# Moving some inverse roots from GpSimd to ScalarE, reordering the first loads, the residual adds and the w_down loads in a linear-attention kernel

## The chip, the core and the metric

The kernel runs on one core of one Trainium2 chip. The metric is the device time of one execution in microseconds (us), the median of several executions. Lower is better. A profile of one execution shows what every engine did: TensorE (PE for its matmuls, PEld for its weight loads), VectorE (DVE), ScalarE (ACT), GpSimd (POOL), and SyncE (SP), which here only issues DMAs. Each engine works through its own instructions in order; semaphores tie them together.

## The reference

The input `x` has 2048 rows of 640 numbers, in bf16. The output is the sum of `x`, of a linear attention and of a small expert branch, both on the normalised rows:

```python
x = A_x
xn = _layernorm(x, axis=-1)            # (x - m) / sqrt(v + 1e-5)
return x + _A_ref(xn, A_wqkv, A_wo) + _B_ref(xn, B_w_r, B_w_gate, B_w_up, B_w_down)

# _A_ref: 32 heads of width 20; phi(t) = where(t > 0, t + 1, exp(t)) + 1e-6
q, k, v = split(x @ wqkv);  pq, pk = phi(q), phi(k)
kv = einsum("bhsd,bhse->bhde", pk, v);  z = einsum("bhsd->bhd", pk)
o = einsum("bhqd,bhde->bhqe", pq, kv) / (einsum("bhqd,bhd->bhq", pq, z) + 1e-6)
return o @ wo

# _B_ref: the 8 rows with the largest router score go through a gated expert
r = x @ w_r;  idx = argsort(-r)[:8];  x_sel = x[idx]
y = (silu(x_sel @ w_gate) * (x_sel @ w_up)) @ w_down * sigmoid(r[idx])
return x.at[idx].add(y)
```

## The kernel before

The 2048 rows are 16 tiles of 128 rows, numbered 0 to 15; a tile's rows lie on the 128 partitions. The program is written out in order (a manual schedule), so the order of the statements is each engine's order. All loads of the long middle part are issued by SP, in the order of the text.

**Start.** ScalarE issues the two pieces of the k weight (`wk`, L88) and the router vector (L89), and then loads its function table (L90). SP issues x tiles 0, 1 and 2 (L92). `load_rest` (L93 to L102) issues the other x tiles and the q weight; its first load waits for a small GpSimd memset.

**Normalisation of a tile.** `stat` (L178) gives mean and variance on VectorE. Then the inverse root of the variance is needed, and there are two helpers for it: `root_act` (L183) does it with two small ScalarE instructions, Ln and Exp, and `root_pool` (L188) with two small GpSimd instructions, an add (L190) and a power (L191). `norm_dve` (L199) or `norm_pool` (L205) writes the normalised tile `xn`. Tiles 0 to 4 are transposed by TensorE (`tr_pe`) and copied out of PSUM by ScalarE and VectorE (`tr_ev`, L234); tiles 5 to 15 by a DMA transpose that SP issues (`tr_dma`, L243). Before, tiles 0 and 1 take their root from ScalarE and tiles 2 to 15 from GpSimd. From tile 5 on, odd tiles are normalised by VectorE and even ones by GpSimd.

**The middle loop** (L481 to L513) has a step for each tile t from 5 to 15. In step t TensorE does the k product of tile t (`k_half` twice), in some steps a unit of the q product (`q_mm`), and the product of the normalised tile t-4 with its phi(k) (`g1`, L279). ScalarE takes exp and relu of k and q from PSUM (`k_act`, `q_act`), VectorE joins them (`k_phi`, L272, and `q_phi`, L302). The same step prepares tile n = t+4: statistics, root, normalisation, transpose. For odd n the normalisation stands at the head of the following step. Weight loads are issued between the steps (`w_jobs`), among them `w_gate`, `w_up`, `wv`, `wo` and four pieces of `w_down` (`load_wd`).

**The residual.** `adds` (L473) turns tiles of `x_sb` in place into x plus its normalised value, with one GpSimd instruction for each tile (`add_s`, L220) and one small one for each group (L474). They stand in steps 12 to 15 and behind the loop (L525). `load_s` (L107) then stores the sums in four pieces to a scratch area in HBM; the last two pieces of `w_down` are issued behind these stores (L528).

**Behind the loop** the router's 8 rows are found, mostly on VectorE, ending with the row numbers `idx_i` (L574). GpSimd gathers the 8 columns into `xsT` (L575 to L577), TensorE does the expert products (L714 with gate and up, L747 with `w_down`), and an indirect DMA adds the result to the scratch area (L763), which is read back into `x_sb` (L768). The last part multiplies each tile by the folded output matrix (`o_mm`, L795) and adds `x_sb`.

Of the kernel before, what the change touches and what calls it, by code (L numbers as in the profile page):

```python
# [37 lines left out]
def kernel(  # L38
# [45 lines left out]

    SP = nc.sync
    wr5 = sb("wr5", [KC, P])
    for lo, hi in ((0, 3), (3, 5)):
        A.dma_start(wk[:, lo:hi, 0:D], wqkv_v[:, lo:hi, D : 2 * D])  # L88
    A.dma_start(wr5[:], B_w_r.rearrange("(kc p) -> kc p", p=P))  # L89
    A.preload_act_table_set("natural_log_exp_and_others")  # L90
    for t in range(3):
        SP.dma_start(x_sb[:, t, :], x_v[:, t, :])  # L92
    def load_rest():  # L93

        G.memset(x_sb[0:1, 3, 0:1], 0.0)
        SP.dma_start(x_sb[:, 3, :], x_v[:, 3, :])
        for a in (4, 6):
            SP.dma_start(x_sb[:, a : a + 2, :], x_v[:, a : a + 2, :])
        SP.dma_start(x_sb[:, 8:12, :], x_v[:, 8:12, :])
        for lo, hi in ((0, 3), (3, 5)):  # L100
            SP.dma_start(wq[:, lo:hi, :], wqkv_v[:, lo:hi, 0:D])
        SP.dma_start(x_sb[:, 12:16, :], x_v[:, 12:16, :])  # L102
# [52 lines left out]
    def router_col():  # L155
        PE.transpose(psb[:, 6, 512 : 512 + KC], wr5[:], ident[0:KC, 0:KC])
        A.copy(wk[:, :, D], psb[:, 6, 512 : 512 + KC])
# [30 lines left out]
    def root_pool(t, n=1):  # L188
        sl = slice(t, t + n)
        G.tensor_scalar_add(t2[:, sl], mv[:, sl, 1], EPS_BF16)  # L190
        G.tensor_tensor(out=rs[:, sl], in0=t2[:, sl], in1=mhalf[:, 0:n], op=ALU.pow)  # L191
# [7 lines left out]
    def norm_dve(t):  # L199
        V.tensor_scalar(  # L200
            out=xn[:, t, :], in0=x_sb[:, t, :], scalar1=mv[:, t, 0:1], scalar2=rs[:, t : t + 1],
            op0=ALU.subtract, op1=ALU.mult,
        )
# [30 lines left out]
    def tr_ev(t, other=A):  # L234
        dst = xnT[:, :, t * P : (t + 1) * P]
        A.copy(dst[:, 0:3, :], psb[:, 7, 0 : 3 * P].rearrange("p (k f) -> p k f", k=3))
        src = psb[:, 6, 0 : 2 * P].rearrange("p (k f) -> p k f", k=2)
        if other is A:
            A.copy(dst[:, 3:, :], src)
        else:  # L240
            V.tensor_copy(dst[:, 3:, :], src)
# [6 lines left out]
    def k_half(t, b):  # L248
        b0 = K_BANK.get(t, 0)
        n = HW + (b if t else 0)  # L250
        for kc in range(KC):
            PE.matmul(  # L252
                ps[:, b0 + b, 0:n],
                lhsT=xnT[:, kc, t * P : (t + 1) * P],
                rhs=wk[:, kc, b * HW : b * HW + n],
                start=(kc == 0), stop=(kc == KC - 1),
            )
# [3 lines left out]
    def k_act(t):  # L261
        b0 = K_BANK.get(t, 0)
        e = evk.tile([P, 2, HW], BF16, tag="ek", name=f"ek{t}")
        r = evk.tile([P, 2, HW], BF16, tag="rk", name=f"rk{t}")
        for b in range(2):
            A.activation(e[:, b, :], ps[:, b0 + b, 0:HW], AF.Exp)  # L266
            A.activation(r[:, b, :], ps[:, b0 + b, 0:HW], AF.Relu)  # L267
        if t:
            A.copy(r_all[:, t : t + 1], ps[:, b0 + 1, HW : HW + 1])
        kev[t] = e, r  # L270
# [39 lines left out]
    def q_ev(u, bank=7):  # L310
        q_act(u, bank)
        q_phi(u)
# [91 lines left out]
    stat(2, 0)  # L404
    norm_dve(1)
    stat(2, 1)
    root_pool(2)
    const_iota()
    k_half(0, 0)
    tr_pe(1)  # L410
    k_half(0, 1)
    tr_ev(1, V)
    router_col()
    k_act(0)
    stat(3, 0)
# [40 lines left out]
    k_half(4, 0)  # L456
    q_act(0)
    k_half(4, 1)
    norm_dve(7)
    tr_dma(7)  # L460
    k_act(4)
    k_phi(3)
    stats2(8)
    root_pool(8)
    norm_pool(8)
# [7 lines left out]
    def adds(t, n):  # L473
        G.tensor_scalar_add(rs1[:, t : t + n], rs[:, t : t + n], 1.0)  # L474
        for i in range(t, t + n):
            add_s(i)

    q_at = {5: (2, 3), 6: (4,), 8: (5,), 10: (6,), 12: (7,)}
    later = {12: [const_grep], 13: [copy_grep]}
    add_at = {12: (0, 2), 13: (2, 2), 14: (4, 3), 15: (7, 3)}  # L480
    for t in range(5, T):  # L481
        qs = q_at.get(t, ())
        n = t + 4
        if 9 < n <= T and n % 2 == 0:
            norm_dve(n - 1)
            tr_dma(n - 1)
            shift(n - 1, 1)
        if qs:
            q_mm(qs[0])
        k_half(t, 0)  # L490
        k_half(t, 1)
        if n < T:
            stats2(n)
            root_pool(n)
            if n % 2 == 0:
                norm_pool(n)
                tr_dma(n)
        if qs:
            q_ev(qs[0])
        k_act(t)  # L500
        if len(qs) > 1:
            q_mm(qs[1])
        g1(t - 4)
        k_phi(t)
        if len(qs) > 1:
            q_ev(qs[1])
        for job in w_jobs.pop(t - 4, []) + later.pop(t, []):
            job()
        if t == 5:
            shift(0, 6)  # L510
            shift(7, 1)
        if t in add_at:
            adds(*add_at[t])  # L513
# [8 lines left out]
                    start=(t == 0 and c in (0, 4)), stop=(t == T - 1), skip_group_check=True,  # L522
                )

    adds(10, 6)  # L525
    for a in range(0, T, 4):
        load_s(a)
    for i in sorted(w_jobs):  # L528
        for job in w_jobs[i]:
            job()  # L530
    PE.transpose(psb[0:T, 1, 0:P], r_all[:], ident[:])
    g1(T - 4)
    r_row = sb("r_row", [T, P], F32)
# [343 lines left out]
```

## Time and profile before

| quantity | value |
|---|---|
| median of 3 runs | 120.12 us (119.82 to 121.27) |
| the profiled execution's own time | 120.3 us |
| its span on the core | 118.6 us |
| granted TensorE clock over the span | 0.999 |
| busy: PE, DVE, ACT, POOL | 108.1, 83.6, 63.6, 51.7 us |
| moved by DMA | 21.77 MB |

The span runs from the first to the last instruction on the core; the 1.7 us between it and the run's own time lie around it. Busy time is an average over stages that have different limits, so the waits are read stage by stage. A row of the timeline gives the start, the duration, the engine, the line, the operation with output and input, the count of merged instructions, and in brackets the idle time before it with what ended it.

### The profile page before, as it was taken

The page shows a single profiled execution, that of the slowest core. Times are in us where ns is not written, and L with a number is a line of the kernel's source. Part 1 is how long each engine was busy: PE and PEld are TensorE (multiplying, and loading weights), DVE is VectorE, ACT ScalarE, POOL GpSimd, SP SyncE. Part 2 cuts the span into 40 slices and gives each one's busy share as a digit, 9 for nine tenths or more (in the row PEclk, how much of TensorE's full clock was granted, in tenths as well). Part 3 has the DMA queues.
Part 4 walks back from the last instruction along what each step waited for, and adds up shares of the span by engine and source line. Part 5 has one row for each costly group of instructions (what it writes and reads, how often), then busy time and mean ns, then how long its engine had stood idle before and what let it go on. Part 6 is the DMA issues. An engine that isn't in the chain of part 4 may idle for free.

```text
span 118.6 us, 2512 instructions
## 1 busy us (share of the span) xinstructions
PE 108.1 (91%) x902; PEld 63.4 (53%) x912; DVE 83.6 (71%) x176; ACT 63.6 (54%) x156; POOL 51.7 (44%) x99
## 2 busy tenths in 40 slices
PE   5778899999999859799999998999999999999980
PEld 2145464546565435365445956665445566677760
DVE  3498797999949495822609959987776568875570
ACT  1438899658585825566219465575977466300000
POOL 7207668283857669899999922000500000000000
PEclk9999999999999999999999999999999999999999
DMA  3999805505827999999999999700059932243333
GB/s 57 377 346 365 283 15 57 112 6 87 288 55 214 276 159 343 249 255 253 182 192 215 378 380 269 128 0 6 3 153 378 358 111 89 94 154 113 114 116 108
DMA packets 22240, 21.77 MB, mean 184 GB/s; under 512 B 8555, under 2 KB 20947, under 8 KB 22227
## 3 DMA queue, kind: packets, MB, share of 16 engines
q1 hardware_dynamic: 20361, 19.58, 61.6%
q10 hardware_dynamic: 1834, 2.01, 4.9%
q8 instruction: 7, 0.11, 0.4%
q14 instruction: 6, 0.05, 0.1%
q0 software_dynamic: 32, 0.01, 0.1%
HBM read 14.42 MB, written 5.25 MB: 166 GB/s over the span
## 4 chain that ended last, share of the span: by engine, by line
PE 29%; DVE 19%; DMA 19%; POOL 17%; issue 7%; ACT 3%; POOLq 2%; SPq 1%
PE ps L795 18%; DMA s_dram<-x_sb 10%; POOL rs L191 7%; DVE stats L179 5%; DMA wv<-in_A_wqkv_dram 5%; PE ps L289 5%; POOL xn L211 4%; POOL t L190 4%; DVE xn L200 4%; DVE pqT L305 4%; DMA x_sb<-in_A_x_dram 4%; DVE pk L274 2%; POOLq L576 2%; DVE mv L181 2%; PE ps L653 2%
## 5 line engine op out<-in xcount | busy, mean ns | idle before, releaser
L252 PE MATMUL ps<-wk,xnT 128*128 128x320 bf16 (+1 forms) x160 | 25.0, 300 | 2.5 <-DMA xnT<-xn 2.4
L289 PE MATMUL ps<-xnT,wq 128*128 128x512 bf16 x93 | 24.0, 379 | 0.7 <-issue 0.2
L795 PE MATMUL ps<-late,pqT 128*128 128x320 bf16 x150 | 21.3, 299 | 0.0
L252 PEld LDWEIGHTS <-xnT 128*128 128x128 bf16 x160 | 15.0, 97 | 11.1 <-DMA xnT<-xn 3.4
L298 ACT ACTIVATE eq<-ps 128x512 bf16<-128x512 f32 x20 | 12.0, 598 | 15.2 <-PE ps L289 15.1
L281 PE MATMUL ps<-pk,xn 128*128 128x512 bf16 x77 | 19.4, 379 | 0.2
L266 ACT ACTIVATE ek<-ps 128x320 bf16<-128x320 f32 x32 | 14.4, 449 | 7.3 <-PE ps L252 7.3
L795 PEld LDWEIGHTS <-pqT 128*128 128x128 bf16 x150 | 14.3, 98 | 6.2 <-issue 0.4
L274 DVE SCALAR_TENSOR_TENSOR pk<-ek,rk 128x640 bf16<-128x640 bf16 x16 | 13.4, 846 | 5.8 <-ACT rk L267 5.7
L804 DVE TENSOR_TENSOR o<-ps,x_sb 128x640 bf16<-128x640 f32 x15 | 12.3, 823 | 6.5 <-PE ps L795 5.6
L305 DVE SCALAR_TENSOR_TENSOR pqT<-eq,rq 128x512 bf16<-128x512 bf16 x20 | 14.1, 706 | 3.9 <-ACT rq L299 3.9
L222 POOL TENSOR_SCALAR x_sb<-x_sb,rs,nm 128x640 bf16<-128x640 bf16 x16 | 15.9, 1008 | 0.5
L179 DVE BATCH_NORM_STATS2 stats<-x_sb 128x6 f32<-128x320 bf16 x32 | 14.4, 481 | 2.3 <-DMA x_sb<-in_A_x_dram 2.3
L289 PEld LDWEIGHTS <-wq 128*128 128x128 bf16 x100 | 9.3, 97 | 10.6 <-issue 1.0
L267 ACT ACTIVATE rk<-ps 128x320 bf16<-128x320 f32 x32 | 14.5, 454 | 0.0
L190 POOL TENSOR_SCALAR t<-mv 128x1 bf16<-128x1 f32 x14 | 5.7, 410 | 15.0 <-DVE mv L181 14.6
L299 ACT ACTIVATE rq<-ps 128x512 bf16<-128x512 f32 x20 | 11.9, 593 | 0.0
L281 PEld LDWEIGHTS <-xn 128*128 128x128 bf16 x80 | 7.6, 97 | 7.6
L191 POOL TENSOR_TENSOR rs<-t,mhalf 128x1 f32<-128x1 bf16 x14 | 10.5, 753 | 1.2
L200 DVE TENSOR_SCALAR xn<-x_sb,mv,rs 128x640 bf16<-128x640 bf16 x11 | 5.3, 479 | 5.8 <-POOL rs L191 5.7
L611 ACT CAST spare<-ps 128x1024 bf16<-128x1024 f32 (+1 forms) x7 | 6.0, 896 | 3.2 <-PE ps L600 3.2
L831 ACT CAST o<-ps 128x160 bf16<-128x160 f32 x1 | 0.3, 292 | 12.7 <-PE ps L821 12.7
(125 smaller groups left out, 114.4 us busy)
## 6 DMA issues: line engine op xcount, KB each, us to landing
s_dram<-x_sb SPq DMA_DIRECT2D x4, 640.0 KB, 9.1
x_sb<-s_dram SPq DMA_DIRECT2D x4, 640.0 KB, 6.8
wd<-in_B_w_down_dram SPq DMA_DIRECT2D x4, 480.0 KB, 9.0
wg<-in_B_w_gate_dram SPq DMA_DIRECT2D x2, 768.0 KB, 4.9
wu<-in_B_w_up_dram SPq DMA_DIRECT2D x2, 768.0 KB, 5.1
x_sb<-in_A_x_dram SPq DMA_DIRECT2D x2, 640.0 KB, 8.4
out_dram<-o SPq DMA_DIRECT2D x8, 160.0 KB, 1.8
out_dram<-o ACTq DMA_DIRECT2D x7, 160.0 KB, 1.8
```

What stands on the lines that cost most here:

```text
L179: V.bn_stats(out=stats[:, t, b, :], in_=x_sb[:, t, b * HW : (b + 1) * HW])
L191: G.tensor_tensor(out=rs[:, sl], in0=t2[:, sl], in1=mhalf[:, 0:n], op=ALU.pow)
L222: G.tensor_scalar(out=x_sb[:, t, :], in0=x_sb[:, t, :], scalar1=rs1[:, sl], scalar2=nm[:, sl], op0=ALU.mult, op1=ALU.add,)
L252: PE.matmul(ps[:, b0 + b, 0:n], lhsT=xnT[:, kc, t * P : (t + 1) * P], rhs=wk[:, kc, b * HW : b * HW + n], start=(kc == 0), stop=(kc == KC ...
L266: A.activation(e[:, b, :], ps[:, b0 + b, 0:HW], AF.Exp)
L267: A.activation(r[:, b, :], ps[:, b0 + b, 0:HW], AF.Relu)
L274: V.scalar_tensor_tensor(out=pk[:, t, :].rearrange("p (b f) -> p b f", b=2), in0=e[:], scalar=1.0, in1=r[:], op0=ALU.min, op1=ALU.add,)
L281: PE.matmul(ps[:, 2 + c, :], lhsT=xn[:, t, c * P : (c + 1) * P], rhs=pk[:, t, 0:512], start=(t == 0), stop=(t == T - 1),)
L289: PE.matmul(ps[:, bank, :], lhsT=wq[:, kc, m * P : (m + 1) * P], rhs=xnT[:, kc, tb * 512 : (tb + 1) * 512], start=(kc == 0), stop=(kc == K ...
L305: V.scalar_tensor_tensor(out=pqT[:, m, tb * 512 : (tb + 1) * 512], in0=e[:], scalar=1.0, in1=r[:], op0=ALU.min, op1=ALU.add,)
L795: PE.matmul(ps[:, b0 + b, 0:HW], lhsT=pqT[:, kc, t * P : (t + 1) * P], rhs=Ms[:, kc, b * HW : (b + 1) * HW], start=(kc == 0), stop=(kc == ...
L804: V.tensor_tensor(out=o_t[:], in0=ps[:, b0 : b0 + 2, 0:HW], in1=x_sb[:, t, :].rearrange("p (b f) -> p b f", b=2), op=ALU.add,)
```

## The change

- The first x tiles: ScalarE issues x tile 1 and then the first piece of `wk`; SP issues x tiles 0 and 2, then the second piece of `wk`, then the router vector.
- Roots: tile 2 takes its root from ScalarE, behind `tr_ev(1)`. In the loop, odd tiles (9, 11, 13, 15) take it from ScalarE at the end of the step, even ones from GpSimd as before. Tiles 3 to 8 stay on GpSimd.
- In front of the loop, `k_act(4)` and `k_phi(3)` stand ahead of `norm_dve(7)` and its transpose.
- The residual adds: one tile each in steps 7, 9 and 11, two in steps 12 and 13, three in 14 and 15, and three behind the loop in place of six.
- The last two pieces of `w_down` are issued ahead of the four stores.

```diff
-    for lo, hi in ((0, 3), (3, 5)):
-        A.dma_start(wk[:, lo:hi, 0:D], wqkv_v[:, lo:hi, D : 2 * D])
-    A.dma_start(wr5[:], B_w_r.rearrange("(kc p) -> kc p", p=P))
+    A.dma_start(x_sb[:, 1, :], x_v[:, 1, :])
+    A.dma_start(wk[:, 0:3, 0:D], wqkv_v[:, 0:3, D : 2 * D])
     A.preload_act_table_set("natural_log_exp_and_others")
-    for t in range(3):
+    for t in (0, 2):
         SP.dma_start(x_sb[:, t, :], x_v[:, t, :])
+    SP.dma_start(wk[:, 3:5, 0:D], wqkv_v[:, 3:5, D : 2 * D])
+    SP.dma_start(wr5[:], B_w_r.rearrange("(kc p) -> kc p", p=P))
...
     stat(2, 1)
-    root_pool(2)
     const_iota()
...
     tr_ev(1, V)
+    root_act(2)
     router_col()
...
     k_half(4, 1)
+    k_act(4)
+    k_phi(3)
     norm_dve(7)
     tr_dma(7)
-    k_act(4)
-    k_phi(3)
...
-    add_at = {12: (0, 2), 13: (2, 2), 14: (4, 3), 15: (7, 3)}
+    add_at = {7: (0, 1), 9: (1, 1), 11: (2, 1), 12: (3, 2), 13: (5, 2), 14: (7, 3), 15: (10, 3)}
...
             stats2(n)
-            root_pool(n)
             if n % 2 == 0:
+                root_pool(n)
                 norm_pool(n)
                 tr_dma(n)
...
         if len(qs) > 1:
             q_ev(qs[1])
+        if n < T and n % 2:
+            root_act(n)
...
-    adds(10, 6)
-    for a in range(0, T, 4):
-        load_s(a)
+    adds(13, 3)
     for i in sorted(w_jobs):
         for job in w_jobs[i]:
             job()
+    for a in range(0, T, 4):
+        load_s(a)
```

## The prediction

> **What bounds the kernel now.** I read the busy times first, then the waits of TensorE, and then a table of stretches, because a wait only counts where TensorE stands still for it.
>
> ```profile
> span 118.6 us, 2512 instructions
> PE 108.1 (91%) x902; PEld 63.4 (53%) x912; DVE 83.6 (71%) x176; ACT 63.6 (54%) x156; POOL 51.7 (44%) x99
> ```
>
> ```profile
> PE ps L252 <- DMA xnT<-xn: 2.4, 2, 1.6
> PE ps L230 <- DVE xn L200: 1.8, 3, 1.2
> PE ps L714 <- POOL xsT L577: 0.4, 1, 0.4
> ...
> DVE xn L200 <- POOL rs L191: 5.7, 6, 1.7
> ```
>
> ```profile
> 0.00:6.46 6.46, 4.02 (x10) 1.19 (x10) 3.11 (x9) 1.78 (x3) 2.96 (x20) 1.00 0.72 229
> 6.46:15.60 9.14, 8.34 (x72) 5.09 (x73) 7.62 (x24) 6.98 (x22) 4.38 (x15) 1.00 0.88 304
> 15.60:41.00 25.40, 25.05 (x140) 13.63 (x140) 20.87 (x49) 18.74 (x56) 16.94 (x26) 1.00 0.51 125
> 41.00:50.00 9.00, 6.50 (x38) 3.56 (x39) 7.62 (x15) 4.12 (x14) 6.86 (x10) 1.00 1.07 247
> 50.00:75.00 25.00, 24.33 (x299) 14.80 (x299) 15.11 (x37) 13.34 (x31) 18.96 (x29) 1.00 1.10 263
> 75.00:115.30 40.30, 39.89 (x354) 25.10 (x353) 29.24 (x47) 18.36 (x33) 1.61 (x1) 1.00 0.39 129
> ```
>
> The columns of the waits are the total, the number and the longest; those of the stretches are from:to, length, busy time of PE, PEld, DVE, ACT and POOL, granted clock, DMA share and GB/s. TensorE is busy 25.05 of 25.40 us, 24.33 of 25.00 and 39.89 of 40.30, so three stretches can hardly be shortened by this change, which leaves its work as it is. It stands still in three places: at the start until 6.46 and a little up to 15.60 (9.14 less 8.34 is 0.80 us), from 41 to 50 (2.5 us, for two DMA transposes), and 0.4 us for the gather at L714. Whatever the change is worth must come out there.
>
> **The change part by part.**
>
> *The first tiles.*
>
> ```profile
> 3.62 0.89 DVE L179 BATCH_NORM_STATS2 stats<-x_sb 128x6 f32<-128x320 bf16 x2 [1.47 <-DMA x_sb<-in_A_x_dram]
> ...
> 4.85 0.29 ACT L185 ACTIVATE lg<-mv,eps 128x1 f32<-128x1 f32 x1 [1.11 <-DVE mv L181]
> 5.18 0.20 ACT L186 ACTIVATE rs<-lg 128x1 f32<-128x1 f32 x1
> ...
> 5.56 0.49 DVE L179 BATCH_NORM_STATS2 stats<-x_sb 128x6 f32<-128x320 bf16 x1 [0.81 <-DMA x_sb<-in_A_x_dram]
> 5.97 0.43 DVE L200 TENSOR_SCALAR xn<-x_sb,mv,rs 128x640 bf16<-128x640 bf16 x1
> ```
>
> Tile 0's root is ready at 5.18 + 0.20 = 5.38, but its normalisation starts at 5.97, because VectorE does tile 1's statistics first and waited 0.81 us for tile 1 until 5.56. Issued first on the other queue, tile 1 no longer stands behind tile 0 and a k weight piece. The statistics then fit right behind tile 0's, which end near 4.8 (3.62 + 0.89 and a sum of 0.21), in the time of the root, and the normalisation starts at about 5.45: 0.52 us sooner. If both tiles now share the engines evenly, tile 0 lands later, at worst at the mean of the two old times, (3.62 + 5.56) / 2 = 4.59, which is 0.97 later and makes this term -0.45. At best tile 0 lands sooner too; the gain has the end 1.47, the whole idle time of the first row. I take 0.52, the row it is nearest to, since tile 0 is still the first of SP's queue. The k weight's second piece now stands behind two x tiles on SP: before, the first k product waited for ScalarE's copy and not for a weight:
>
> ```profile
> 7.37 0.52 PEld L252 LDWEIGHTS <-xnT 128*128 128x128 bf16 x5 [0.52 <-ACT xnT L236]
> ```
>
> The bytes ahead of it on both queues together stay the same, so I cost it at nothing; if that cover is gone, TensorE waits here for the weight. The router vector goes behind it and is needed by one transpose after that product. SP's next load, tile 3, waits for a GpSimd memset as before.
>
> *The root of tile 2.*
>
> ```profile
> 8.66 0.48 ACT L236 COPY xnT<-ps 128x384 bf16<-128x384 bf16 x1 [0.92 <-PE ps L230]
> 9.30 0.58 POOL L191 TENSOR_TENSOR rs<-t,mhalf 128x1 f32<-128x1 bf16 x1
> 9.91 0.67 DVE L200 TENSOR_SCALAR xn<-x_sb,mv,rs 128x640 bf16<-128x640 bf16 x1 [0.45 <-POOL rs L191]
> ```
>
> On the old clock, ScalarE ends its copy at 8.66 + 0.48 = 9.14; Ln and Exp by the rows above take 0.29 + 0.20, with three hand-overs of 0.04 (5.14 to 5.18) it is 9.75, against 9.91: 0.16 sooner. The normalisation took 0.67, against 0.43 for tile 0's, while GpSimd built its index constants beside it; those constants now run sooner, as GpSimd has no root of tile 2 to wait for. That gives up to 0.24 more, together 0.4. Behind the two instructions on ScalarE stand the router's copy and tile 0's exp and relu, which TensorE needs only at tile 3. I take 0.4 of the 0.80 us in which TensorE still waits in this stretch; the ends are 0 and 0.8.
>
> The Trainium skill, "SBUF — State Buffer", section "Summary: rules for kernel authors", has it that a VectorE instruction in a two-port mode and a GpSimd instruction block each other for the whole instruction. The pair 0.67 and 0.43 agrees, and by that rule the residual adds in steps 7, 9 and 11 would lie in front of VectorE in return.
>
> *Tile 7 and phi(k) of tile 3.*
>
> ```profile
> 20.34 0.57 POOL L191 TENSOR_TENSOR rs<-t,mhalf 128x1 f32<-128x1 bf16 x1
> 20.95 0.45 DVE L200 TENSOR_SCALAR xn<-x_sb,mv,rs 128x640 bf16<-128x640 bf16 x1 [0.77 <-POOL rs L191]
> 21.31 0.82 DVE L274 SCALAR_TENSOR_TENSOR pk<-ek,rk 128x640 bf16<-128x640 bf16 x1
> ```
>
> VectorE waited 0.77 us for GpSimd's root, and phi(k) came after. Now phi(k), which needs nothing new, fills that wait; the root is ready at 20.91 as before, so what follows comes 0.7 us sooner. VectorE's waits in this stretch are mostly those for GpSimd's roots (5.7 us in six), and the next of them comes after tile 10's statistics, so these start 0.52 + 0.4 + 0.7 = 1.6 us sooner. The ends for this step are 0 and 0.77.
>
> *The transposes.*
>
> ```profile
> 28.61 0.87 DVE L179 BATCH_NORM_STATS2 stats<-x_sb 128x6 f32<-128x320 bf16 x2
> 31.93 1.56 POOL L211 TENSOR_SCALAR xn<-x_sb,rs,nm 128x640 bf16<-128x640 bf16 x1
> 33.52 1.20 SPq L244 DMA_TRANSPOSE xnT<-xn  x1
> 34.48 0.45 DVE L200 TENSOR_SCALAR xn<-x_sb,mv,rs 128x640 bf16<-128x640 bf16 x1 [1.74 <-POOL rs L191]
> 34.77 1.08 SPq L105 DMA_DIRECT2D wg<-in_B_w_gate_dram  x2
> 35.95 5.08 SPq L244 DMA_TRANSPOSE xnT<-xn  x2
> 42.73 1.21 PEld L252 LDWEIGHTS <-xnT 128*128 128x128 bf16 x10 [2.12 <-DMA xnT<-xn]
> ...
> 49.69 0.39 PEld L252 LDWEIGHTS <-xnT 128*128 128x128 bf16 x4 [1.31 <-DMA xnT<-xn]
> ```
>
> This is the chain to see. Tile 11's root is what VectorE waits 1.74 us for, and that wait goes; but tile 11 is normalised at 34.93 and its transpose is issued at 35.95, because SP first issues tile 10's transpose (33.52, at the end of 31.93 + 1.56 = 33.49) and two weight pieces. Tile 10 has an even number: its root stays on GpSimd. So the removed wait is not what frees TensorE at 42.73. What moves that transpose is tile 10's statistics at 28.61, 1.6 us sooner by the sum above. The transpose of tile 11 then lands at about 42.73 - 1.6 = 41.1. TensorE would be there at 42.73 - 1.6 (its longest wait) - 0.9 (the first two terms) = 40.2, still waits 0.9, and goes on 1.6 us sooner than before. The other wait, 2.4 - 1.6 = 0.8 us at 49.69, is for tile 13, behind two pieces of `w_up`. Here the earlier root helps, since tile 12's statistics follow tile 11's normalisation; but the transfers ahead keep their length. Its ends are 0 and 0.8; I take 0.2, nearer to the transfers.
>
> *What ScalarE takes on.* Five roots at 0.49 are 2.5 us. ScalarE is busy 18.74 of 25.40, so they find room; behind each stand the next exp and relu, for which TensorE waits last. GpSimd loses five roots and gets three more small sums.
>
> *The adds and the gather.*
>
> ```profile
> 61.78 5.61 POOL L222 TENSOR_SCALAR x_sb<-x_sb,rs,nm 128x640 bf16<-128x640 bf16 x6
> 65.40 0.15 DVE L574 CAST idx_i<-cols 128x1 int32<-128x1 f32 x1
> 67.34 1.27 POOL L577 COPY xsT<-xnT 128x5 bf16 x3
> 73.34 1.42 PEld L714 LDWEIGHTS <-xsT 128*32 128x32 bf16 x40 [0.69 <-POOL xsT L577]
> ```
>
> The gather starts at 67.34, behind the sixth add, though the row numbers are there at 65.55. Three adds at 5.61 / 6 = 0.93 are gone from here, 2.8 us, so the gather starts 67.34 - 65.55 = 1.8 us sooner against its neighbours. TensorE's wait for it is only 0.4, so 0.4 is the gain; then TensorE's own work is next. The expert's last product waits for nothing but its weight loads and the chain before it:
>
> ```profile
> 79.30 0.81 PEld L747 LDWEIGHTS <-late 128*32 128x32 bf16 x48
> ```
>
> No wait for `w_down` is shown, so its earlier issue gains nothing. The stores go behind it; their user, the indirect add, comes after L747, 12 us after the last add at 67.39, which covers them.
>
> *Sum.* 0.52 + 0.4 + 0.7 + 0.2 + 0.4 = 2.2 us off the profiled run's 120.3 gives 118.1. That run stands 0.2 above the median of 120.12, from which the same sum gives 117.9. I predict **118.0 us**. From no change this kernel's measurement can tell about 2%, here 117.7 and 122.5.
>
> **The rivals.**
>
> *All the waits go.* If the DMA queue has a gap that the earlier issue closes, tile 13's transpose keeps up: 2.2 + 0.6 = 2.8, and if tile 11's remaining 0.9 goes too, 3.7: 116.5 to 117.4, say 117.0. For it speaks the DMA share of 0.51 before 41; against it 1.07 after.
>
> *The late statistics stay where they are.* If VectorE gives back the 0.7 at tile 7, for the three adds put beside it (3 x 0.93 = 2.8 us of GpSimd) or for GpSimd's slow pieces, the transposes come only 0.9 sooner: 0.9 + 0.4 = 1.3, 118.9. For it speaks the 1.56 us normalisation, against 0.93 for an add of the same size; against it VectorE's 1.74 us of idle time in the later steps.
>
> *The change does not do what it says at the start.* Tile 0 shares the sixteen DMA engines with tile 1 and lands later; between the ends 0.52 and -0.45 that is a term near 0, and 118.5. The Trainium skill, "DMA: Bandwidth & Descriptors", section "Issuing engines are not separate DMA queues", says that transfers issued by several engines run on the same DMA engines and interleave, so that only issue time is saved. By that rule this case would be the likelier one for tile 0; the trace of before has no two x tiles in flight on two queues and does not decide it.
>
> *Slower than before: ScalarE is held up by its new waits.*
>
> ```profile
> 30.90 0.43 ACT L267 ACTIVATE rk<-ps 128x320 bf16<-128x320 f32 x1
> 31.84 0.21 DVE L181 BATCH_NORM_AGGREGATE mv<-stats 128x2 f32<-128x12 f32 x1
> 32.73 0.60 ACT L298 ACTIVATE eq<-ps 128x512 bf16<-128x512 f32 x1 [1.34 <-PE ps L289]
> ```
>
> At the end of step 7 ScalarE is done at 31.33, tile 11's variance is there at 32.05, and ScalarE's next work at 32.73. Ln and Exp fit in by 0.2 us. If the variance comes later, Ln stops everything behind it: the q and k pieces in PSUM stay, and TensorE cannot refill the banks. Some 0.5 us more pass before that hurts. Four tiles with a variance 1.25 us later would cost 4 x (1.25 - 0.7) = 2.2 and eat the gain; with 1.5 us it is 3.2, and the run takes 121.1. VectorE's place in the order ahead of phi(k) of the step speaks against it.
>
> **How the numbers follow.** The forecast has 0.45 (117.5 to 118.6), all waits gone 0.20, late statistics 0.18, the shared start 0.10, and held-up ScalarE 0.07. The range goes from the middle of the first rival, 116.9, up past the late statistics with a lost start term, 118.9 + 0.5, to 119.6. Faster by over 2% needs 117.7: most of the first rival and a third of the forecast, 0.18 + 0.15 = 0.33. Slower by over 2% is only the far end of the last rival and what I don't see, 0.04. Within 2%: 0.63.
>
> **What would show it.** Right: no wait of VectorE for tile 1, tile 0 normalised at about 5.45; TensorE's wait at tile 11 about 0.9; tile 10's transpose issued near 31.9; no wait at L714, with the gather starting right behind `idx_i`. Wrong: a wait of TensorE for `wk` at its first k product; Ln (L186 by then) with long waits and TensorE waiting for PSUM behind it; VectorE's instructions longer in steps 7, 9 and 11; the two transposes landing as late as before.

## The result and the profile after

| quantity | before | after |
|---|---|---|
| median of 19 runs each, side by side | 120.68 us | 118.63 us |
| ratio, with its 95% interval | | 0.9844 [0.9818, 0.9869] |
| the profiled execution's own time | 120.3 us | 118.64 us |
| its span | 118.6 us | 116.9 us |

The change makes the kernel 1.6% faster: 1.88 us off 120.68 by the ratio, inside the 2% taken as no change for this kernel, and inside the range of 116.9 to 119.6. The forecast was 118.0. In the profiles of two experiments the granted TensorE clock falls to 0.50 for 3.4 us, from 42.9 us in e2_roots and from 49.7 us in f2_gate_later, so their rows from there on are read only where the text says so.

Line numbers in the profile after are 1 higher up to the loop and 3 higher behind it: L201 is `norm_dve`, L253 `k_half`, L717 the expert products. First the head of the page, then the rows of the chain of waits that answer to those of before (total, number, longest):

```profile
span 116.9 us, 2517 instructions
PE 108.2 (93%) x912; PEld 63.4 (54%) x912; DVE 83.2 (71%) x176; ACT 65.5 (56%) x166; POOL 47.6 (41%) x92
```

```profile
PE ps L253 <- DMA xnT<-xn: 1.8, 1, 1.8
...
PE ps L231 <- DVE xn L201: 1.0, 1, 1.0
PE ps L523 <- issue: 0.6, 1, 0.6
...
DVE xn L201 <- POOL rs L192: 0.7, 2, 0.5
```

VectorE's waits for GpSimd's roots fell from 5.7 us to 0.7. But TensorE's wait for transposes fell only from 2.4 us to 1.8: of its two, one went and the other, 1.6 before, is longer. The wait for the gather (0.4) is gone, and a new one of 0.6 has "issue" as its releaser: nothing in the profile ends it. The same stretches as before:

```profile
0.00:6.46 6.46, 4.20 (x15) 1.55 (x16) 3.42 (x10) 1.79 (x4) 3.87 (x23) 1.00 0.72 239
6.46:15.60 9.14, 8.81 (x74) 5.26 (x72) 7.93 (x25) 8.12 (x28) 3.31 (x11) 1.00 0.86 297
15.60:41.00 25.40, 24.44 (x138) 13.18 (x136) 23.71 (x54) 19.40 (x58) 16.98 (x25) 1.00 0.63 130
41.00:50.00 9.00, 8.01 (x49) 4.70 (x50) 4.79 (x9) 5.50 (x18) 8.46 (x12) 1.00 1.00 332
50.00:75.00 25.00, 24.36 (x313) 15.00 (x312) 15.33 (x38) 12.89 (x30) 13.37 (x22) 1.00 1.00 236
75.00:115.30 40.30, 38.36 (x332) 23.73 (x330) 28.00 (x45) 17.76 (x32) 1.61 (x1) 1.00 0.40 132
```

TensorE does 0.65 us more work before 15.60 (4.20 + 8.81 against 4.02 + 8.34), loses 0.61 between 15.60 and 41, where the wait at tile 11 now begins, and does 1.51 more from 41 to 50. The rest follows from the timeline, in the order of the path. At the start, on VectorE:

```profile
3.78 0.89 DVE L180 BATCH_NORM_STATS2 stats<-x_sb 128x6 f32<-128x320 bf16 x2 [1.63 <-DMA x_sb<-in_A_x_dram]
4.83 0.44 DVE L180 BATCH_NORM_STATS2 stats<-x_sb 128x6 f32<-128x320 bf16 x1
5.57 0.45 DVE L201 TENSOR_SCALAR xn<-x_sb,mv,rs 128x640 bf16<-128x640 bf16 x1 [0.30 <-ACT rs L187]
...
9.22 0.45 DVE L201 TENSOR_SCALAR xn<-x_sb,mv,rs 128x640 bf16<-128x640 bf16 x1
```

Tile 1 is there right behind tile 0, and tile 0 is normalised at 5.57 instead of 5.97; over all the profiles it is 5.46 to 5.72 with the new start and 5.76 to 6.10 with the old one. Tile 0 itself lands 0.16 us later (3.78 against 3.62); over all the profiles it lands at 3.67 to 3.92 with the new start and at 3.35 to 3.75 with the old one. Tile 2's normalisation ends at 9.67 instead of 10.58. The first q product starts 0.88 us sooner (14.89 against 15.77). Then tile 7:

```profile
19.46 0.99 POOL L192 TENSOR_TENSOR rs<-t,mhalf 128x1 f32<-128x1 bf16 x1
20.49 0.45 DVE L201 TENSOR_SCALAR xn<-x_sb,mv,rs 128x640 bf16<-128x640 bf16 x1 [0.46 <-POOL rs L192]
...
27.42 0.87 DVE L180 BATCH_NORM_STATS2 stats<-x_sb 128x6 f32<-128x320 bf16 x2
```

GpSimd's power for tile 7 took 0.99 us where it took 0.57 before, now that phi(k) of tile 3 runs beside it. The trace of before already holds such a pair, for tile 10:

```profile
30.20 0.82 DVE L274 SCALAR_TENSOR_TENSOR pk<-ek,rk 128x640 bf16<-128x640 bf16 x1
30.45 1.00 POOL L191 TENSOR_TENSOR rs<-t,mhalf 128x1 f32<-128x1 bf16 x1
```

Tile 10's statistics start 1.19 sooner in the changed kernel (28.61 before). The transposes, and TensorE at tile 11 and at tile 13:

```profile
32.26 1.20 SPq L245 DMA_TRANSPOSE xnT<-xn  x1
33.51 1.08 SPq L106 DMA_DIRECT2D wg<-in_B_w_gate_dram  x2
34.69 2.79 SPq L245 DMA_TRANSPOSE xnT<-xn  x2
37.54 1.13 SPq L106 DMA_DIRECT2D wu<-in_B_w_up_dram  x2
38.77 4.66 SPq L245 DMA_TRANSPOSE xnT<-xn  x2
...
41.99 1.54 PE L253 MATMUL ps<-wk,xnT 128*128 128x320 bf16 x10 [1.77 <-DMA xnT<-xn]
...
47.97 1.53 PE L253 MATMUL ps<-wk,xnT 128*128 128x320 bf16 x10
```

Tile 11's transpose is issued 1.26 us sooner (34.69 against 35.95) but lands only 0.74 sooner (41.99 against 42.73, the starts of TensorE's product, which waits for it in both): it takes 7.3 us instead of 6.8. Tile 12's is now issued right behind it, and so `w_up` and tile 13's transpose go out 3.5 and 4.1 us sooner than before; the wait at tile 13 is gone and its k product starts at 47.97 instead of 49.69, 1.72 sooner. That lead is kept to the end of the loop, and then part of it is lost:

```profile
62.23 0.15 DVE L577 CAST idx_i<-cols 128x1 int32<-128x1 f32 x1
...
68.19 0.62 PE L523 MATMUL ps<-pk,xn 128*128 128x128 bf16 x8
69.44 1.95 PE L523 MATMUL ps<-pk,xn 128*128 128x128 bf16 x32 [0.64 <-issue]
...
71.65 0.67 PE L717 MATMUL ps<-wg,xsT 128*32 128x384 bf16 x12
```

The expert products start at 71.65 instead of 73.34 without waiting for the gather. The lead there is 1.73 (from the loop) + 0.41 (the gather's wait) + 0.16 (a stall of before at 68.75) - 0.64 (the new stall) = 1.66; the rows give 1.69, and the span is 1.7 shorter. The gather itself does not start right behind `idx_i`, as the prediction had it, but at 63.62, after GpSimd stood idle for 2.09 us; it is still early enough for TensorE.

### The profile page after: what moved, and what is told of

Read it like the earlier page. It is cut to its first block, busy times and chain, and to the rows that moved or that the text cites. A ratio compares the mean times of both kernels' runs of the same rounds, so it can differ in the third digit from the quotient of the medians.

```text
span 116.9 us, 2517 instructions
## 1 busy us (share of the span) xinstructions
PE 108.2 (93%) x912; PEld 63.4 (54%) x912; DVE 83.2 (71%) x176; ACT 65.5 (56%) x166; POOL 47.6 (41%) x92
## 4 chain that ended last, share of the span: by engine, by line
PE 62%; ACT 13%; DVE 6%; DMA 6%; POOL 5%; issue 3%; POOLq 0%
PE ps L798 18%; PE ps L290 12%; PE ps L282 10%; PE ps L253 8%; DMA xnT<-xn 6%; PE ps L523 4%; ACT rq L300 3%; ACT ek L267 2%; ACT eq L299 2%; ACT rk L268 2%; DVE pqT L306 2%; PE ps L656 2%; DVE xn L201 2%; PE ps L717 1%; PE ps L603 1%
## 5 line engine op out<-in xcount | busy, mean ns | idle before, releaser
L253 PE MATMUL ps<-wk,xnT 128*128 128x320 bf16 (+1 forms) x160 | 25.0, 300 | 1.9 <-DMA xnT<-xn 1.8
L290 PE MATMUL ps<-xnT,wq 128*128 128x512 bf16 x100 | 24.7, 379 | 0.2
L253 PEld LDWEIGHTS <-xnT 128*128 128x128 bf16 x160 | 15.1, 97 | 10.4 <-DMA xnT<-xn 2.3
L275 DVE SCALAR_TENSOR_TENSOR pk<-ek,rk 128x640 bf16<-128x640 bf16 x16 | 13.9, 879 | 7.5 <-ACT rk L268 7.5
L191 POOL TENSOR_SCALAR t<-mv 128x1 bf16<-128x1 f32 x9 | 3.8, 427 | 13.6 <-DVE mv L182 13.3
L192 POOL TENSOR_TENSOR rs<-t,mhalf 128x1 f32<-128x1 bf16 x9 | 6.8, 759 | 0.8
L624 DVE TENSOR_TENSOR pqT<-pqT,ps 128x1024 bf16<-128x1024 bf16 (+1 forms) x5 | 4.9, 1003 | 2.5 <-PE ps L603 2.5
```

The lines of the kernel that those rows point to most:

```text
L253: PE.matmul(ps[:, b0 + b, 0:n], lhsT=xnT[:, kc, t * P : (t + 1) * P], rhs=wk[:, kc, b * HW : b * HW + n], start=(kc == 0), stop=(kc == KC ...
L275: V.scalar_tensor_tensor(out=pk[:, t, :].rearrange("p (b f) -> p b f", b=2), in0=e[:], scalar=1.0, in1=r[:], op0=ALU.min, op1=ALU.add,)
L290: PE.matmul(ps[:, bank, :], lhsT=wq[:, kc, m * P : (m + 1) * P], rhs=xnT[:, kc, tb * 512 : (tb + 1) * 512], start=(kc == 0), stop=(kc == K ...
```

## The experiments

Each verdict is a ratio to the kernel before, run beside it (120.34 to 120.45 us), with its 95% interval; the gain in us is worked out from that ratio.

### Each part alone

e1_start has the change's first hunk alone, and e2_roots the moved roots alone:

```diff
-    for lo, hi in ((0, 3), (3, 5)):
-        A.dma_start(wk[:, lo:hi, 0:D], wqkv_v[:, lo:hi, D : 2 * D])
...
+    A.dma_start(x_sb[:, 1, :], x_v[:, 1, :])
+    A.dma_start(wk[:, 0:3, 0:D], wqkv_v[:, 0:3, D : 2 * D])
...
-    for t in range(3):
+    for t in (0, 2):
...
```

> The kernel before with the new order of the first loads alone. Queue theory (after the start TensorE is held where the transposes of tiles 11 and 13 land, and these follow tile 10's and tile 12's preparation and what SP issues ahead of them): tile 0 is normalised near 5.57 instead of 5.97, all that follows moves by the same 0.4 us, the waits at tiles 11 and 13 stay 1.6 and 0.8; the time falls by 0.4 us. Rival (absorbed): the transposes land as late as before for the sake of the DMA queue, the wait at tile 11 grows by 0.4 and the time does not change.

```diff
-    root_pool(2)
...
+    root_act(2)
...
-            root_pool(n)
             if n % 2 == 0:
+                root_pool(n)
...
+        if n < T and n % 2:
+            root_act(n)
```

> The kernel before with the five roots on ScalarE alone. Queue theory: tile 2 is normalised 0.3 to 0.5 us sooner; tile 11's transpose stays behind tile 10's and the two w_gate pieces, so TensorE still waits about 1.6 us for it; tile 12 is prepared sooner, the w_up pieces go out sooner and the wait for tile 13 (0.8) goes: the time falls by 1.1 to 1.3 us. Root theory (the rival: TensorE pays for VectorE's waits for the roots): both waits go with VectorE's 1.7 us waits, and the time falls by 2.5 us or more.

e2b_odd is e2_roots without the two lines on tile 2.

> The kernel before with the roots of tiles 9, 11, 13 and 15 alone by ScalarE at the end of the step, tile 2's root left on GpSimd. With e2_roots (1.06 us faster than before) it splits the gain. Theory of the prediction: tile 2's root is worth 0.4 and the odd roots the rest, so 0.6 faster here, 119.9 us. Rival (tile 2's gain is lost behind the late statistics of tile 8, where VectorE waits for tile 7's root): all of the gain is the odd roots', 1.0 faster, 119.4 us, with TensorE's wait at tile 13 gone. Rival (the gain is tile 2's): no more than 0.3 faster.

e3_phi moves only `norm_dve(7)` and its transpose behind `k_act(4)` and `k_phi(3)`; e4_adds has only the new steps of the residual adds:

```diff
-    norm_dve(7)
-    tr_dma(7)
     k_act(4)
     k_phi(3)
+    norm_dve(7)
+    tr_dma(7)
```

> The kernel before with phi(k) of tile 3 ahead of tile 7's normalisation alone. Queue theory, with the two engines in each other's way: GpSimd's power for tile 7 takes 0.99 instead of 0.57 us beside phi(k), VectorE gains 0.3 us of the 0.77, tile 10's transpose goes out 0.3 sooner and the time falls by 0.3 us. Rival (as predicted blind): VectorE gains 0.7 and the time falls by 0.7 us. Rival (absorbed): no change.

```diff
-    add_at = {12: (0, 2), 13: (2, 2), 14: (4, 3), 15: (7, 3)}
+    add_at = {7: (0, 1), 9: (1, 1), 11: (2, 1), 12: (3, 2), 13: (5, 2), 14: (7, 3), 15: (10, 3)}
...
-    adds(10, 6)
+    adds(13, 3)
```

> The kernel before with the moved residual adds alone. Gather theory: the gather starts behind idx_i instead of behind the sixth add, the wait at L714 (0.4 us) goes and the time falls by 0.4 us. Rival (the new stall of TensorE within the 128x128 products in front of it, 0.6 us with no releaser, comes with the earlier gather): that stall appears here too and the time rises by 0.2 us. Rival (the adds in steps 7, 9 and 11 hold up GpSimd's roots, which here are still its own): the waits at tiles 11 and 13 grow and the time rises by 0.5 us or more.

| kernel | ratio to before | gain | forecast for the part |
|---|---|---|---|
| e1_start | 0.9964 [0.9926, 1.0001] | 0.43 us | 0.52 |
| e2_roots | 0.9912 [0.9864, 0.9961] | 1.06 us | 0.4 + 0.2 |
| e2b_odd | 0.9880 [0.9836, 0.9925] | 1.44 us | 0.2 |
| e3_phi | 1.0008 [0.9973, 1.0044] | -0.10 us | 0.7 |
| e4_adds | 0.9970 [0.9940, 1.0000] | 0.36 us | 0.4 |

The four parts together (e1 to e4) give 0.43 + 1.06 - 0.10 + 0.36 = 1.75 us, near the 1.88 of the whole. That sum is no proof that the parts are independent: two of them, as shown below, take the same wait of TensorE. The roots of the odd tiles alone carry most of the gain; the 0.6 expected for them lies outside their interval (0.90 to 1.98 us), the rival's 1.0 inside. That tile 2's root adds nothing to them can't be settled: the intervals of e2_roots and e2b_odd overlap. In the timeline of e2b_odd, on TensorE and on the queue:

```profile
35.81 3.12 SPq L244 DMA_TRANSPOSE xnT<-xn  x2
...
43.28 1.54 PE L252 MATMUL ps<-wk,xnT 128*128 128x320 bf16 x10 [2.25 <-DMA xnT<-xn]
...
49.26 1.53 PE L252 MATMUL ps<-wk,xnT 128*128 128x320 bf16 x10
```

Tile 11's product is 0.55 us *later* than before (42.73) and its wait is longer, yet tile 13's starts 0.43 sooner (49.69 before), without a wait. So the odd roots do not work through tile 11; they work through tiles 12 and 13, whose transposes and the `w_up` pieces between them go out sooner. That is 0.43 of the 1.0 us by which this span is shorter. Another 0.41 is the wait for the gather: with four roots fewer GpSimd ends the six adds behind the loop, left at their old place, at 64.04 instead of 67.39, before `idx_i` is there (64.65), and TensorE's expert products start at 72.31 without a wait.

```profile
58.78 5.26 POOL L222 TENSOR_SCALAR x_sb<-x_sb,rs,nm 128x640 bf16<-128x640 bf16 x6
...
65.99 0.20 POOL L579 COPY xsT<-xnT 128x5 bf16 x1 [1.94 <-DVE junk L679]
...
72.31 1.00 PE L716 MATMUL ps<-wg,xsT 128*32 128x384 bf16 x20
```

The last 0.16 is the stall of before at 68.75, which is not there. In e2_roots tile 7 is normalised at 20.57 instead of 20.87 here, but tile 11's product starts at 43.26 against 43.28: that lead ends in TensorE's wait.

The gain of 0.7 for phi(k) is excluded by e3_phi. Its rows show where it went, GpSimd's power and VectorE:

```profile
20.31 0.99 POOL L191 TENSOR_TENSOR rs<-t,mhalf 128x1 f32<-128x1 bf16 x1
...
21.34 0.45 DVE L200 TENSOR_SCALAR xn<-x_sb,mv,rs 128x640 bf16<-128x640 bf16 x1 [0.46 <-POOL rs L191]
```

Of the 0.82 us that phi(k) needs, 0.42 comes back as a longer power (0.99 against 0.57). Tile 10's statistics start 0.34 sooner; no gain in time is left of that.

### What holds tile 11's transpose, and what its wait is worth

f2_gate_later moves the second and third `w_gate` piece of the changed kernel from just ahead of tile 11's transpose to step 8, behind it:

```diff
-        w_jobs[1 + i] = [lambda i=i: kcw(wg, B_w_gate, 2 * i, min(2 * i + 2, KC))]
-        w_jobs[4 + i] = [lambda i=i: kcw(wu, B_w_up, 2 * i, min(2 * i + 2, KC))]
+        w_jobs.setdefault((1, 4, 4)[i], []).append(lambda i=i: kcw(wg, B_w_gate, 2 * i, min(2 * i + 2, KC)))
+        w_jobs.setdefault(4 + i, []).append(lambda i=i: kcw(wu, B_w_up, 2 * i, min(2 * i + 2, KC)))
```

> The changed kernel with the second and third w_gate piece issued in step 8, behind the transposes of tiles 11 and 12 instead of just ahead of them. Queue theory (what is issued ahead of a transpose sets when it lands): tile 11 lands in about 4.5 us instead of 7.3, TensorE's wait of 1.77 us there goes; tile 13's transpose now stands behind four weight pieces and lands near 49, a wait of about 1 us there: 117.9 us. Rival (the landing of 7.3 us is the transposes' own, the second one issued right behind the first): the wait of 1.77 stays, 118.6 us.

The DMA view of this kernel, for the issue of tile 11's transpose (the last column is us to landing), and TensorE's timeline:

```profile
xnT<-xn SPq DMA_TRANSPOSE x1, 2.6
```

```profile
49.50 2.73 PE L253 MATMUL ps<-wk,xnT 128*128 128x320 bf16 x10 [3.30 <-DMA xnT<-xn]
```

With no weight ahead of it the transpose lands in 2.6 us, not 7.3, and the wait of 1.77 at tile 11 is gone. So the queue theory holds for tile 11: 4.7 of the 7.3 us are the 1.15 MB of `w_gate` ahead. The price was put too low: tile 13 now waits 3.30 us behind these bytes and those of `w_up`, 1.5 more than was saved, and behind this wait ten products take 2.73 us instead of 1.53, at the lower clock. The ratio to before is 0.9971 [0.9927, 1.0014] against 0.9844 of the changed kernel, so this order costs 1.5 us.

f4_early moves the weights the other way, into the gaps of the queue before 34 us:

```diff
     load_rest()
+    load_wg(0)
...
     tr_dma(6)
+    load_wg(1)
...
     tr_dma(8)
+    load_wg(2)
...
-        w_jobs[4 + i] = [lambda i=i: kcw(wu, B_w_up, 2 * i, min(2 * i + 2, KC))]
+        w_jobs[(1, 2, 4)[i]] = [lambda i=i: kcw(wu, B_w_up, 2 * i, min(2 * i + 2, KC))]
...
```

> The changed kernel with the weight pieces issued earlier, where the queue has gaps: first w_gate piece behind the x loads, second behind the transpose of tile 6, third behind that of tile 8, w_up in steps 5, 6 and 8, none in step 7 ahead of the transpose of tile 11; w_v, w_o and w_down two steps sooner. Queue theory: the wait of 1.77 us at tile 11 goes and none returns, 116.9 us. Rival (the transposes of tiles 5 to 8 land later behind the gate pieces and TensorE waits there): 118.6 us or more, with a new wait at the k product of one of tiles 5 to 8. Rival (the tail after 75 us is set by something else, as the gather or the issue stall, that takes the gain): 118.0 us.

It measured 0.9767 [0.9723, 0.9811], 2.8 us faster than before and 0.9 faster than the changed kernel: about half of the 1.7 expected. In its profile the wait at tile 11 is gone and none returns at tiles 5 to 8, so the first rival falls. How much of that the weights did is not shown by this profile alone: its first products ran at half speed (see the last section), and TensorE comes to tile 11 at 41.69 instead of 40.22. One of 0.98 us appears at tile 15, whose transpose now stands behind `w_o`.

f3_root7 leaves the weights alone and takes tile 7's root from ScalarE too:

```diff
-    root_pool(7)
...
     k_act(4)
+    root_act(7)
     k_phi(3)
     norm_dve(7)
```

> The changed kernel with the root of tile 7 by ScalarE (Ln and Exp behind the k copies of tile 4) instead of GpSimd. Theory that GpSimd's power, 0.99 us beside phi(k) of tile 3, holds VectorE up by 0.46: tile 7 is normalised near 20.0 instead of 20.49, and the transposes of tiles 10 and 11 are issued 0.4 sooner; 118.2 us. Rival (the transpose of tile 11 lands by the weights ahead of it, whatever its issue): k of tile 11 starts where it did, 118.6 us.

VectorE's rows of this kernel:

```profile
19.37 0.81 DVE L275 SCALAR_TENSOR_TENSOR pk<-ek,rk 128x640 bf16<-128x640 bf16 x1
20.11 0.43 DVE L201 TENSOR_SCALAR xn<-x_sb,mv,rs 128x640 bf16<-128x640 bf16 x1
```

Now there is no wait behind phi(k), and the step does what the prediction had asked of it. Tile 10's transpose is issued at 31.49 (32.26 in the changed kernel, "near 31.9" forecast), tile 11's at 33.92, and TensorE has no wait for a transpose at all: tile 11's product starts at 40.71, 1.28 sooner than in the changed kernel. The kernel measured 117.79 us, 0.9782 [0.974, 0.9824], better than the 118.2 expected. By the ratios that is 0.75 us faster than the changed kernel, more than the wait of 0.46; the two intervals just overlap.

### The adds and the stall without a releaser

f1_oldadds is the changed kernel with the old steps of the adds:

```diff
-    add_at = {7: (0, 1), 9: (1, 1), 11: (2, 1), 12: (3, 2), 13: (5, 2), 14: (7, 3), 15: (10, 3)}
+    add_at = {12: (0, 2), 13: (2, 2), 14: (4, 3), 15: (7, 3)}
```

> The changed kernel with the scaled adds back at their old steps (12 to 15 and the end). Step theory: the earlier adds are worth what they gave alone, 0.36 us; so 119.0 us here against 118.6 of the changed kernel, and TensorE waits again about 0.5 us for GpSimd's gather at the expert products. Rival (contention): adds in steps 7, 9 and 11 lengthen VectorE's normalisations and hold the transposes up; then this kernel is not slower than the changed one, 118.6 or less. Rival (the gain was taken by the 0.64 us stall of TensorE without a releaser in the second half of the G columns 512 to 639): 118.6, with that stall gone and the gather's wait back.

0.9875 [0.9837, 0.9912], 118.84 us: 0.3% slower than the changed kernel by the ratios, with overlapping intervals. The wait for the gather, which two of the three theories above had coming back, did not. TensorE stalled 0.96 us ahead of it with no releaser, but that is not why: the last column is copied by 69.83, and the products, at 71.19, would have started at 70.23 without the stall. As in e2b_odd GpSimd is done with the six adds early, at 62.77, before `idx_i` (63.10):

```profile
57.60 5.17 POOL L223 TENSOR_SCALAR x_sb<-x_sb,rs,nm 128x640 bf16<-128x640 bf16 x6
64.33 0.74 POOL L580 COPY xsT<-xnT 128x5 bf16 x1 [1.56 <-DVE zm L679]
```

The new steps of the adds are thus worth 0.36 alone (e4_adds, whose interval ends at 1.0000), but next to the moved roots the profile shows nothing left for them to gain. Do they cost something, as the contention rival has it? In f1_oldadds tile 11's transpose, issued at 34.84, lands after 5.7 us, and TensorE waits 0.20 for it instead of 1.77; but g3_stores_first (below), which has the adds in steps 7, 9 and 11, lands it after 5.8. So the adds alone do not make the difference, and the times do not decide it either.

The stall stands ahead of the same product, the ninth of its half, in the changed kernel, in f1_oldadds and in f3_root7. The DMA queue q8, which carries 16 KB blocks of kind "instruction", has one block shortly before. In the DMA view of the changed kernel for 67.0 to 67.1 us it is this row (packets, MB, share):

```profile
q8 instruction: 1, 0.02, 64.9%
```

| kernel | block read at | TensorE at the product | stall | goes on, after the read |
|---|---|---|---|---|
| changed kernel | 67.0 | 68.80 | 0.64 | 69.44, 2.4 |
| f1_oldadds | 66.7 | 68.02 | 0.96 | 68.98, 2.3 |
| f3_root7 | 65.9 | 67.52 | 0.82 | 68.34, 2.4 |
| before | 67.1 | 70.6 | 0 | 3.5 |
| f4_early | 66.2 | 69.6 | 0 | 3.4 |

TensorE passes that product no sooner than 2.3 us after the read; a kernel that comes later does not stall. In f2_gate_later, where the clock is back at 1.00, the block is read at 69.8 and the ninth product starts at 72.11, again 2.3 later, with 0.1 lost ahead of it. That fits a wait of TensorE for its own code. The Trainium skill, "Runtime: NRT & Kernel Launch", section "Instruction fetch mechanics", says that each engine's instructions come in 16 KiB blocks over a DMA queue of their own and that this is mostly hidden; the blocks on q8 agree; if this is such a wait, up to 0.96 us was not hidden here. Two kernels test it: eight matmuls more for TensorE at the start, and the stores ahead of the last `w_down` pieces again.

```diff
     warm(NWARM + 3, 0)
+    for i in range(8):
+        PE.matmul(ps[:, 0, 0:16], lhsT=zw[:, 0:P], rhs=zw[:, 0:16], start=True, stop=True)
```

> The changed kernel with eight matmuls of 16 columns more behind the five that warm TensorE up, inside its wait of 1.0 us for tile 0. Code theory: the stall of 0.64 us stands where a block of TensorE's code begins, so eight instructions more move it from the ninth product of the second half of the G columns 512 to 639 to the first; its length is between 0.64 (the read moves with it) and 1.26 us (the read comes when it came); the time stays within 0.3 us of 118.6. Rival (the stall is a wait for something that the ninth product reads, as a buffer or a bank): it stays ahead of the ninth product. Rival (chance of one execution): no stall.

```diff
+    for a in range(0, T, 4):
+        load_s(a)
     for i in sorted(w_jobs):
         for job in w_jobs[i]:
             job()
-    for a in range(0, T, 4):
-        load_s(a)
```

> The changed kernel with the stores of the scaled rows ahead of the last two w_down pieces again, as before the change. Theory that w_down's place costs nothing (its cover: the down product comes after 75 us, the gather does not read it): 118.6 us, and TensorE's read of code and stall as in the changed kernel. Rival (w_down behind the stores is late): TensorE or GpSimd's gather waits for wd by some tenths, 119.0 us. Rival (the stores moved behind w_down are what delays TensorE's code): stall of 0.64 gone, 118.0 us.

g2_eight_more: 118.12 us, 0.9823 [0.9764, 0.9882], and no stall at all; the block is read at 65.5, 1.5 us sooner. So my expectation of a shifted stall fell, and what came is what the rival of chance had named. If the eight instructions did move the read, that speaks for code and against a buffer, but it is one execution. g3_stores_first: 118.07 us, 0.9796 [0.9751, 0.9841], no stall either, the read at 65.1, and no wait for `w_down`. So the part "`w_down` ahead of the stores" gains nothing. No stall and 118.0 us is what the last rival had, by which this part costs some tenths by way of the read; it stays open, since the intervals overlap and the stall went in g2_eight_more too, with the stores in their new place. What sets the moment of the read is not settled.

### Both repairs together

g1_early_root7 is the changed kernel with tile 7's root on ScalarE and the weights of f4_early, with `w_o` behind tile 15's transpose:

```diff
-        7: [lambda: load_cols(wv, 0, 3, 2 * D)], 8: [lambda: load_cols(wv, 3, 5, 2 * D)],
-        9: [load_wo],
+        5: [lambda: load_cols(wv, 0, 3, 2 * D)], 6: [lambda: load_cols(wv, 3, 5, 2 * D)],
+        8: [load_wo],
...
-        w_jobs[10 + j] = [lambda j=j: load_wd(j)]
+        w_jobs[9 + j] = [lambda j=j: load_wd(j)]
```

> The changed kernel with both repairs: root of tile 7 by ScalarE, and the weights issued earlier as in f4_early, with w_o moved behind the transpose of tile 15 (where f4_early waited 0.98 us) and w_down one step sooner than in the changed kernel. Theory that TensorE's stall in the second half of the G columns 512 to 639 (0.82 us in f3_root7) is a wait for its own code, whose read stands behind data in full queues: with the queues empty 2 us sooner the read comes sooner, no stall is left, and no wait for a transpose: 117.0 us against 117.8 of f3_root7. Rival (the stall stands at that instruction whatever the queues hold): 117.8 us. Rival (the two repairs take the same wait, and TensorE is the bound behind it): 117.8 us, with neither stall nor wait in the profile.

**116.41 us, 0.9654 [0.9612, 0.9696]**: 3.5% faster than before, below the changed kernel's interval. Its stretches:

```profile
15.60:41.00 25.40, 24.82 (x142) 13.72 (x141) 23.49 (x53) 19.59 (x61) 14.94 (x22) 1.00 0.81 177
41.00:50.00 9.00, 9.00 (x56) 5.29 (x55) 6.45 (x10) 6.05 (x20) 8.46 (x10) 1.00 0.94 230
50.00:75.00 25.00, 25.00 (x317) 14.94 (x315) 17.29 (x41) 13.68 (x30) 13.86 (x24) 1.00 0.84 202
```

TensorE is busy for all of 41 to 75 us. The block of code is read at 64.1 and the stall is gone; of the 1.0 us by which the span is shorter than f3_root7's (114.8 against 115.8), 0.82 is that stall and 0.21 lies before the end of the loop. From here on TensorE's own work is the bound, but for the start and 0.48 us for a q bank at 20.19, behind ScalarE's two new instructions.

## Why the prediction was right and where it was not

The total was near: 1.66 us between the profiled executions against 2.2 forecast, with the median 0.6 above the number. The division among the parts was partly wrong, and that the errors nearly cancel is luck.

- **First tiles: 0.52 forecast; 0.40 in the profile, 0.43 alone.** The mechanism is as described: no wait of VectorE for tile 1. Tile 0 lands 0.16 later, with tile 1 in flight beside it, and VectorE then waits 0.30 for the root. The shared-start rival, with a term near 0, falls in the profiles, though the interval of e1_start touches 0. The second `wk` piece, costed at nothing, was never waited for.
- **Root of tile 2: 0.4 forecast; 0.51 in the profile** (0.91 at the end of its normalisation less 0.40 from the start). Both halves are there: no wait, and 0.45 instead of 0.67 long. Together the first two terms were forecast at 0.92, and the q product starts 0.88 sooner.
- **Tile 7: 0.7 forecast; 0.31 in the profile** (1.19 at tile 10's statistics less 0.88), nothing measurable alone. This step failed. "The root is ready at 20.91 as before" held the root's time fixed while a long VectorE instruction was moved beside it. The power became 0.42 longer, as the row at 30.45 of the kernel before (1.00 beside phi(k)) could have told. The rival of the late statistics had the place right; of its two causes the adds were not it, and GpSimd's slow pieces come near, with a power for the normalisation it named. f3_root7 shows the step without that collision.
- **Tile 11: landing at 41.1 with a wait of 0.9 forecast; 41.99 and 1.77 measured.** The working "42.73 - 1.6" held the landing's length fixed, but it grew by 0.5 us, and the issue was 0.34 less early than 1.6. That 1.6 was the number from which the rest of the path was reckoned, and it is the largest error of the sum: 0.74 came out.
- **Tile 13: 0.2 forecast, between 0 and 0.8; the whole 0.82 came.** I took the end nearer to the transfers, reasoning that "the transfers ahead keep their length". They were issued 3.5 us sooner, because tile 12's transpose stands ahead of them in SP's order, and tile 12's statistics on VectorE no longer stand behind tile 11's normalisation, which waited for GpSimd's late root (they start at 32.40 instead of 34.92). "The removed wait is not what frees TensorE" was true of tile 11 only; at tile 13 it is what frees TensorE, by e2b_odd. The errors at tiles 11 and 13 cancel, by luck: 1.6 + 0.2 forecast, 1.72 measured at tile 13.
- **Adds and gather: 0.4 forecast; 0.41 in the profile, 0.36 alone.** The size came out, but the sum took this term as the adds' own. In e2b_odd and f1_oldadds the wait is gone with the adds at their old place, so the moved roots alone take it too. Then 0.64 was lost to a stall that the profile of before could not show, because TensorE came to that product after its code did. In the profile this stall is most of what the forecast missed: without it, 1.66 would have been 2.3.
- **The adds beside VectorE:** they do not lengthen the normalisations that the rival feared for. Tile 11's takes 0.92 us in the changed kernel (0.45 before), but it takes 0.92 in f1_oldadds too, which has no add there; what runs beside it, in the changed kernel from 30.72 to 32.23, is GpSimd's normalisation of tile 10. It is an add that is held up: one takes 1.72, the shortest 0.87.
- **ScalarE held up by Ln** (the slower case): not seen. No new wait of TensorE for ScalarE is in the profile of the changed kernel; one of 0.48 us came only with tile 7's root, in f3_root7 and g1_early_root7.

## What to carry to other kernels

Where transposes and weight loads share one queue, reckon with the order of issue: a wait removed on a compute engine pays at the first transfer that it lets out sooner, and that can be two tiles further on than the tile whose wait it was. A lead that reaches an engine standing in front of a landing is worth nothing until the landing moves too; here early issue of the weights into gaps was worth 0.9 us, of the size of the compute edits (0.75 for tile 7's root, 1.44 for the odd ones alone). Two edits that are each worth something alone can take the same wait, so look for the second one's wait in the profile of the first. And when a long instruction is moved into another's waiting time, ask whether the thing waited for keeps its own duration: other places of the same trace may already show the pair.

## What the runs showed of the hardware

- A GpSimd power on 128x1 elements took 0.57 us by itself and 0.99 to 1.00 beside VectorE's scalar_tensor_tensor of 128x640, 1.26 where both started together (28.86 in f3_root7). In that one, in the changed kernel, in e3_phi and in the kernel before (30.45) it ends 0.41 to 0.45 us after VectorE's instruction. The Trainium skill, "SBUF — State Buffer", section "Summary: rules for kernel authors", has the second of a VectorE and a GpSimd instruction blocked until the first ends, where VectorE is in a two-port mode, or has two SBUF inputs while GpSimd reads SBUF; phi(k) has two inputs, and these ends fit such blocking, but no run here tells which case it is.
- A DMA transpose of one tile lands in 2.6 us on an idle queue. Behind the same 1.15 MB of weights it took between 5.7 us (f1_oldadds) and 7.7 us (e2_roots); what makes that difference is open.
- TensorE's stall of 0.64 to 0.96 us ahead of one product, 2.3 to 2.4 us after a 16 KB block on the instruction queue, in three of the kernels.
- In some executions the first products run at about half speed for some 4 us. In e1_start and in the changed kernel:

```profile
7.47 1.54 PE L253 MATMUL ps<-wk,xnT 128*128 128x320 bf16 x5
```

```profile
6.99 0.85 PE L253 MATMUL ps<-wk,xnT 128*128 128x320 bf16 x5
```

The stretches of both have a granted clock of 1.00 here, but the trace's clock records do not reach back so far: the first, of 1.00, begins at 9.81 us in e1_start and at 4.73 in the changed kernel. From 10.46 on e1_start too has 0.85 for five such products. The profiled executions of g3_stores_first and f4_early show it too (first records at 9.90 and 10.67; in all the others between 4.27 and 5.89): three of nine profiles with the new start and none of five with the old. In g3_stores_first tile 7 is normalised 1.1 us later than in the changed kernel (21.59 against 20.49), and yet tile 11's product starts 0.4 sooner, at 41.60: what was lost at the start came out of the waits for transposes. The Trainium skill, "TensorE: Matmul & The Clock Gate", section "What's actually happening", has TensorE's clock at half until some 3.4 us of sustained activity; the factor of 1.8 and the late first records agree with it, but whether the new start makes it likelier was not tried.
- At the end of TensorE's two longest waits, of 2.52 us until 43.26 in e2_roots and of 3.30 us until 49.50 in f2_gate_later, the clock records go to 0.50 for 3.4 us, from 42.91 and from 49.67 us on; the wait of 2.25 us in e2b_odd has no such record.
